# A gated recurrence into a gated feed-forward layer: y transposed by TensorE for all slabs, the cap as minimum and maximum, and a new order of all steps

## The chip, the cores and the metric

The kernel runs on one core of a Trainium2 chip. Its time is device microseconds of one execution. A second execution was taken by the hardware profiler; all rows below come from that one.

## The reference, cut to what matters

There are 4 batches, 8 heads, 768 time steps and 48 values a head. Each head has a complex state of 48 x 48 that decays by a complex factor for each row, and takes up the outer product of k and v:

```
mag = sqrt(a_re^2 + a_im^2);  scale = minimum(mag, 0.999) / (mag + 1e-6)
ar, ai = a_re * scale, a_im * scale
for t in range(768):
    S_re, S_im = ar[t] * S_re - ai[t] * S_im + outer(k[t], v[t]),  ar[t] * S_im + ai[t] * S_re
    y[t] = q[t] @ S_re
x   = y as (3072 tokens, 384)
out = (sigmoid(x @ w_gate) * (x @ w_val)) @ w_out      # 384 -> 1536 -> 384, float32
```

## The kernel before, in words

**Tiling.** Time is cut into six chunks of 128 steps. A *slab* m is one chunk c of one batch b, with all 8 heads: 128 time steps on the partitions, 384 columns; m counts 4c + b, so there are 24. Slabs come in seven groups (`SIZES`: 4, 4, 4, 4, 4, 2, 2), which share the steps on the decays; slabs come in pairs w = m // 2 for the feed-forward layer.

**The steps of a group and a slab**, by the names that the planner uses. Decays: `lr`, `la` load a_re and a_im; `sq`, `add` give the squared magnitude, `lnm` its logarithm, `lh` the cap. In groups 2 to 6 (`SPLIT`) `lh` caps the logarithm and writes a float16 high part (line 631), and `ll` on VectorE the remainder (line 640); in groups 0 and 1 the cap comes before the logarithm (line 622). `cl` sums the logarithms over time by a matmul with a triangle, `ee` takes exponentials, `scr` and `rbe` carry the last row's decay through memory, `arr` multiplies it. Angles: `lna`, `inv`, `r`, `atan`, `hop`, `th`, `tl`, then sums by `ct`, rounding by `r16` and `nid`, and `cr`, `ab`, `cs` for carry, cosine and sine. Products: `lk`, `lq`, `lv` load k, q, v; `v16` and `qke` scale them; `ks`, `qs` turn them by the angles. For slabs 9 to 23 (`CROSSED`) `xk` and `xq` transpose them by a crossbar DMA (line 881), for the others `tp` on TensorE and `qkT`, a copy. `sc` makes scores, `mst` masks them, `u`, `x16`, `kv`, `P` carry the state, and `y` (lines 995 and 997) puts both parts together in a bank of PSUM.

**Around the change.** `y16` (lines 1008 to 1011) copies y to float16. Then the feed-forward layer wants it transposed, in a tile `xt` of the pair. For slabs in `YCROSSED`, 4 to 23, step `xt` is a crossbar DMA from SP's queue (line 1016). For the others `xp` makes three 128 x 128 transposes on TensorE into a bank (line 1029) and `xt` copies them out, on VectorE or ScalarE (line 1035). When both slabs of a pair have their `xt`, `pg` and `pv` multiply by w_gate and w_val (line 1054, twelve matmuls for a block of 256 hidden columns, six each), `tanh` and `p` gate, `po` multiplies by w_out (line 1093), `ot` copies out, `st` stores.

**What sets the order.** A planner wrote it out beforehand: `TIMES` has a due time for each step, `Plan.order` sorts all steps by it, and every engine carries out its own steps in that order; a step that waits holds all that stand behind it on its engine. The due times are the planner's numbers, and no measurement. SP issues all loads, `scr`, `rbe`, `car`, the crossbar DMAs and the stores in one queue; the weights and `hop` are issued by GpSimd. `HOME` names the engine of a step that has a choice (v VectorE, a ScalarE, g GpSimd), one letter a slab or pair; `SLOTS` says which of a few buffers each tile gets, the eight banks of PSUM (`ps`) among them. `WARM` puts dummy matmuls of zeros ahead of some TensorE steps (line 1132). Activation tables are loaded where the next function needs another set.

Of the kernel before, what the change touches and what calls it, by code (L numbers as in the profile page):

```python
# [10 lines left out]
ALU = mybir.AluOpType  # L11
# [17 lines left out]
YCROSSED = range(4, 24)  # L29
# [5 lines left out]
    "sq": "aaavvvvaavaaaaaaavvaaaaa",  # L35
    "add": "vgvvvggggggggggggggggggg",
    "lh": "vgvgggggggvg",
    "r": "vvgggvgggggv",
    "v16": "ggavgvggvggvggaggaavvavv",
    "qke": "vggggggggggggggggggggggg",  # L40
    "th": "aaaaggggvgav",
    "ab": "vavvvaaavvavaavaaaaaavva",
    "u": "ggggggggggggggvggggg",
    "x16": "gagggggaggagggva",
    "y16": "aavvvavaavvvaaaavavvvvvv",
    "xt": "vvvavvvvvvvvvvvvvvvvvvvv",
    "ot": "vvavvvvaavvaaavvaavvaaaaa",
# [17 lines left out]
    "sq": [
        4.48, 10, 6.32, 8.16, 17.85, 17.86, 21.38, 29.97, 51.59, 50.73, 56.79,
        63.29, 82.29, 91.4, 88.28, 87.26, 107.64, 104.58, 114.27, 114.29,
        147.67, 152.47, 176.52, 173.69],
    "add": [
        7.2, 10.92, 7.68, 9.03, 19.38, 20.6, 30.47, 32.67, 56.38, 63.25,  # L70
        65.53, 66.21, 87.89, 92.17, 90.8, 88.18, 110.42, 111.34, 128.31,
        116.63, 162.03, 164.86, 177.13, 178.13],
    "lna": [
        11.97, 33.75, 64.73, 92.51, 117.97, 165.5, 180.57],
    "lh": [
        11.96, 9.67, 20.61, 32.68, 69.79, 70.41, 97.82, 98.99, 132.8, 140.86,
        165.93, 180.53],
    "lnm": [
        13.56, 33.16, 66.22, 93.79, 129.94, 165.92, 179.6],
    "inv": [  # L80
        12.16, 33.76, 70.86, 106.34, 117.98, 166.8, 181.9],
    "r": [
        16.38, 13.68, 37.9, 37.89, 74.86, 73.97, 108.49, 109.1, 118.24,
        134.35, 172.6, 183.16],
    "cl": [
        15.08, 16.37, 19.88, 20.63, 33.77, 38.14, 39.84, 33.97, 77.53, 79.36,
        71.95, 78.08, 101.69, 105.47, 107.63, 106.65, 138.38, 138.71, 143.08,
        142.1, 168.69, 170.09, 197.48, 195.63],
    "ee": [
        19.39, 19.87, 20.58, 21.37, 37.16, 43.83, 41.98, 37.17, 81.07, 81.68,  # L90
        72.77, 82.28, 102.22, 107.65, 109.34, 108.48, 140.04, 143.11, 144.33,
        143.41, 169.29, 172.61, 201.81, 196.64],
# [73 lines left out]
    "mst": [  # L166
# [215 lines left out]
def kernel(  # L382
# [184 lines left out]
    for g, n in enumerate(SIZES):  # L567
# [595 lines left out]
```

## Time and profile before

| | us |
|---|---|
| median of 3 runs | 315.61 (314.3 to 316.31) |
| profiled execution | 316.14 |
| its span, first to last instruction | 314.4 |
| TensorE matmuls busy | 237.2 (75%) |
| VectorE busy | 207.1 (66%) |
| ScalarE busy | 200.6 (64%) |
| GpSimd busy | 147.8 (47%) |

The mean granted clock of TensorE is 0.908 of full speed. Busy time is a share of the whole span; in the rows, PE is TensorE, PEld its weight loads, DVE VectorE, ACT ScalarE, POOL GpSimd, SPq the sequencer that issues DMAs. "out<-in" names tiles by the program's names. A time in brackets is how long the engine stood idle before the row, and what ended it.

### The profile page before, as it was taken

What the parts mean: (1) busy time and instruction counts of PE and PEld (TensorE: products, weight loads), DVE (VectorE), ACT (ScalarE), POOL (GpSimd) and SP (SyncE); (2) the same over time, 40 slices, a digit from 0 to 9 for tenths busy, and PEclk for the clock granted to TensorE, in tenths of its full rate; (3) what the DMA queues carried; (4) which work ended last, traced back from release to release, by engine and by line L of the source; (5) the groups of instructions that cost most, each with busy time, mean ns of one, the idle gap of its engine ahead of it and who ended that gap; (6) DMA issues with size and microseconds to landing.
All of it is one profiled execution on the core that took longest, in us unless ns stands there. A gap on an engine that the chain in (4) does not pass through costs nothing.

```text
span 314.4 us, 5826 instructions
## 1 busy us (share of the span) xinstructions
PE 237.2 (75%) x2178; PEld 175.5 (56%) x2178; DVE 207.1 (66%) x334; ACT 200.6 (64%) x313; POOL 147.8 (47%) x140
## 2 busy tenths in 40 slices
PE   0094899995997937598968649779759699779396
PEld 0042766794674626366845427547547477467284
DVE  3569998994887737477978628648626469567131
ACT  3688997797677945579877719568556376512032
POOL 3218773499754579627299443057214350240000
PEclk9998799999599996979999959887969789979989
DMA  8999969969957593693994799394493618263401
GB/s 160 217 214 193 202 91 164 139 115 151 203 98 152 125 174 71 129 190 87 216 163 94 116 177 220 74 177 100 87 205 75 142 25 183 57 124 83 125 2 52
DMA packets 191309, 42.24 MB, mean 134 GB/s; under 512 B 184200, under 2 KB 191280, under 8 KB 191280
## 3 DMA queue, kind: packets, MB, share of 16 engines
q1 hardware_dynamic: 187136, 38.29, 64.4%
q0 software_dynamic: 4144, 3.56, 7.9%
q8 instruction: 17, 0.28, 0.4%
q14 instruction: 12, 0.10, 0.1%
HBM read 30.77 MB, written 4.78 MB: 113 GB/s over the span
## 4 chain that ended last, share of the span: by engine, by line
PE 26%; DMA 12%; SPq 6%; DVE 4%; issue 3%; POOL 3%; ACT 3%; DVEq 0%; POOLq 0%; ACTq 0%
PE banks L1054 15%; PE banks L1093 6%; DMA xt<-y 4%; DMA rbe<-scr 3%; DMA qkT<-kst 2%; SPq L561 2%; SPq L1016 2%; PE banks L922 2%; SPq L881 1%; DMA out_dram<-ot 1%; DMA a<-in_a_im_dram 1%; DVE p L1072 1%; DVE mst L937 1%; DVE y L523 1%; POOL state L951 1%
## 5 line engine op out<-in xcount | busy, mean ns | idle before, releaser
L1054 PE MATMUL banks<-xt,wg 128*128 128x256 f16 x432 | 63.3, 295 | 20.0 <-DMA xt<-y 15.9
L1065 ACT ACTIVATE g<-banks 128x512 f16<-128x512 f32 x72 | 42.0, 596 | 45.1 <-PE banks L1054 35.7
L1054 PE MATMUL banks<-xt,wv 128*128 128x256 f16 x432 | 64.6, 295 | 4.6 <-DMA xt<-y 3.9
L1054 PEld LDWEIGHTS <-wg 128*128 128x128 f16 x432 | 44.3, 105 | 33.1 <-issue 19.1
L732 POOL TENSOR_TENSOR qk<-qk,ee 128x768 f32<-128x768 f32 x23 | 43.6, 1896 | 40.2 <-DMA qk<-in_q_dram 23.8
L1072 DVE SCALAR_TENSOR_TENSOR p<-g,banks 128x512 f16<-128x512 f16 x72 | 48.0, 681 | 17.9 <-ACT g L1065 12.4
L1093 PE MATMUL banks<-wo,p 128*128 128x384 f16 (+1 forms) x300 | 56.2, 327 | 0.0
L1054 PEld LDWEIGHTS <-wv 128*128 128x128 f16 x432 | 44.7, 106 | 19.6 <-issue 7.4
L937 DVE TENSOR_TENSOR mst<-banks,msk_t 128x512 f16<-128x512 f32 x48 | 32.2, 684 | 22.9 <-PE banks L922 21.4
L1126 ACT ACT_TABLE_LOAD x31 | 39.8, 1283 | 0.5
L1093 PEld LDWEIGHTS <-p 128*128 128x128 f16 x300 | 28.5, 100 | 15.0 <-issue 1.2
L860 DVE TENSOR_TENSOR kst<-qk,banks 128x768 f16<-128x768 f32 x24 | 22.7, 947 | 8.6 <-POOL qk L732 7.8
L600 POOL TENSOR_TENSOR lm<-sq 128x384 f32<-128x384 f32 x20 | 20.7, 1039 | 16.4 <-ACT sq L592 10.1
L922 PEld LDWEIGHTS <-qkT 128*128 128x128 f16 x192 | 15.1, 108 | 23.7 <-DMA qkT<-kst 12.2
L592 ACT ACTIVATE sq<-a 128x768 f32<-128x768 f32 x17 | 14.4, 845 | 15.4 <-DMA a<-in_a_im_dram 10.7
L860 DVE TENSOR_TENSOR qst<-qk,banks 128x768 f16<-128x768 f32 x24 | 22.7, 945 | 0.0
L922 PE MATMUL banks<-qkT,qkT 128*128 128x128 f16 x120 | 12.6, 244 | 12.3 <-DMA qkT<-kst 10.5
L631 POOL TENSOR_SCALAR lh<-lm 128x768 f16<-128x768 f32 x7 | 19.4, 2780 | 3.7 <-ACT lm L613 3.5
L679 ACT ACTIVATE ee<-banks 128x384 f32<-128x384 f32 x24 | 11.8, 492 | 12.6 <-PE banks L671 11.4
L667 PE MATMUL banks<-lm,wl_t 128*128 128x384 f32 x16 | 7.9, 612 | 15.6 <-ACT lm L613 15.6
L656 POOL TENSOR_TENSOR a<-a 128x768 f32<-128x768 f32 x8 | 15.3, 1925 | 5.8 <-ACT a L650 5.8
L807 DVE TENSOR_SCALAR r<-banks 128x384 f16<-128x384 f32 x24 | 13.1, 551 | 6.7 <-PE banks L792 6.6
(91 smaller groups left out, 407.4 us busy)
## 6 DMA issues: line engine op xcount, KB each, us to landing
a<-in_a_re_dram SPq DMA_DIRECT2D x24, 192.0 KB
a<-in_a_im_dram SPq DMA_DIRECT2D x24, 192.0 KB
v<-in_v_dram SPq DMA_DIRECT2D x24, 192.0 KB
qk<-in_k_dram SPq DMA_DIRECT2D x24, 192.0 KB
qk<-in_q_dram SPq DMA_DIRECT2D x24, 192.0 KB
out_dram<-ot SPq DMA_DIRECT2D x23, 192.0 KB
wg<-in_moe_w_gate_dram POOLq DMA_DIRECT2D x3, 384.0 KB, 6.5
wv<-in_moe_w_val_dram POOLq DMA_DIRECT2D x3, 384.0 KB, 5.3
```

The lines of the kernel that those rows point to most:

```text
L600: home("add", m).tensor_tensor(out=T[LM][:, s], in0=T[SQ][:, 0], in1=T[SQ][:, 1], op=ALU.add)
L631: home("lh", w).tensor_scalar(out=T[LH][:, 0, i:j], in0=T[LM][:, i:j], scalar1=LNCAP, scalar2=1.0, op0=ALU.min, op1=ALU.mult)
L656: home("r", w).tensor_tensor(out=T[A][:, 1, i:j], in0=T[A][:, 1, i:j], in1=T[A][:, 0, i:j], op=ALU.mult)
L732: home("qke", m).tensor_tensor(out=T[QK], in0=T[QK], in1=T[EE], op=ALU.mult)
L860: nc.vector.tensor_tensor(out=T[SL][i].rearrange("p h (r x) -> p h r x", r=2)[:, :, :, 0:D], in0=heads(T[QK][:, i]).unsqueeze(2) .broadcas ...
L922: nc.tensor.matmul(sc[:, 4 * hf * both + i], kt, qt, start=True, stop=True)
L937: nc.vector.tensor_tensor(out=T[MS][:, :n_], in0=T[SC], in1=msk_t.unsqueeze(1).broadcast_to([L, n_, L]), op=ALU.mult)
L1054: nc.tensor.matmul(T[ACC][:, r], wt[:, j, f0:f0 + 128], T[XT][:, :, j], start=(j == 0), stop=(j == 2))
L1065: nc.scalar.activation(out=T[G16], in_=T[PG], func=FT.Tanh, scale=0.5)
L1072: nc.vector.scalar_tensor_tensor(out=T[PT][:, 2 * fp:2 * fp + 2], in0=T[G16], scalar=1.0, op0=ALU.add, in1=T[PV], op1=ALU.mult)
L1093: nc.tensor.matmul(T[PO][:, :wd], T[PT][:, fb, s0:s0 + L], wo16[:, fb, c0:c0 + wd], start=(fb == 0), stop=(fb == NFB - 1))
L1126: nc.scalar.preload_act_table_set(SETS[key[1]])
```

## The change

The range of slabs whose y goes by the crossbar becomes empty, so slabs 4 to 23 take the two steps that slabs 0 to 3 had. The cap of the split groups does a minimum with the logarithm's limit and then a maximum with -200 in place of a multiplication by 1. Homes, due times, buffers and dummies of all steps are new: 37 dummies in place of 26, other slabs for most homes, and the last group (slabs 22, 23) now ends before the one of slabs 20, 21.

```diff
-YCROSSED = range(4, 24)
+YCROSSED = ()
 HOME = {
...
-    "lh": "vgvgggggggvg",
+    "lh": "gvgggggvvggv",
...
-    "y16": "aavvvavaavvvaaaavavvvvvv",
-    "xt": "vvvavvvvvvvvvvvvvvvvvvvv",
+    "y16": "vaavavvvaavvavvvaaaaaaaa",
+    "xt": "vvavvvvvavvvvvvavavaavav",
...
 TIMES = {
...
     "y": [
-        34.81, 41.97, 39.99, 45.62, 66.83, 67.24, 81.71, 88.4, 100.63, 105.59,
-        110.39, 114.91, 136.7, 137.43, 151.36, 150.3, 165.49, 168.28, 178.14,
-        177.15, 201.18, 201.82, 215.25, 217.61],
+        35.34, 52.95, 39.91, 41.45, 65.88, 66.29, 85.49, 85.97, 103.07,
+        106.19, 121.6, 118.72, 132.83, 136.14, 152.51, 152.46, 168.42, 166.57,
+        182.06, 183.12, 217.78, 216.07, 201.29, 205.6],
...
     "xp": [
-        37.3, 42.95, 45.44, 49.24],
+        44.07, 56.12, 42.3, 42.62, 68.09, 69.89, 88.51, 88.68, 108.61, 108.44,
+        123.73, 124.6, 135.27, 138.5, 156, 156.01, 170.3, 170.13, 184.83,
+        184.99, 219.5, 219.88, 205.59, 205.67],
     "xt": [
-        37.75, 43.32, 45.48, 49.61, 70.42, 70.43, 84.3, 91.38, 103.71, 108.47,
-        117.28, 117.29, 138.62, 139.05, 153.27, 153.28, 168.9, 170.11, 180.62,
-        180.79, 203.15, 205.16, 218.68, 218.75],
+        44.44, 57.32, 43.28, 44.11, 69.86, 70.69, 89.51, 89.61, 109.11,
+        109.53, 124.78, 125.88, 137.6, 138.93, 156.04, 156.51, 171.79, 171.81,
+        187.61, 187.64, 219.87, 220.19, 205.64, 205.97],
...
 WARM = {
-    ('sc', 0, 1): 3,
-    ('sc', 1, 1): 1,
-    ('kv', 2): 1,
-    ('kv', 1): 1,
-    ('sc', 4, 1): 1,
-    ('pg', 0, 2): 9,
-    ('kv', 4): 5,
-    ('sc', 7, 0): 5,
+    ('ct', 3): 8,
+    ('ct', 1): 1,
+    ('sc', 0, 0): 4,
+    ('sc', 0, 1): 10,
+    ('y', 0): 2,
+    ('pv', 1, 0): 4,
+    ('pv', 1, 3): 1,
+    ('cl', 10): 7,
 }
...
             def e2(T, LM=LM, LH=LH, i=i, j=j, w=w):
                 home("lh", w).tensor_scalar(
                     out=T[LH][:, 0, i:j], in0=T[LM][:, i:j], scalar1=LNCAP,
-                    scalar2=1.0, op0=ALU.min, op1=ALU.mult)
+                    scalar2=-200.0, op0=ALU.min, op1=ALU.max)
```

## Rows read from the trace of the kernel before

**Rows 1.** The page: busy time and instructions of TensorE, granted clock in tenths.
```profile
PE 237.2 (75%) x2178; PEld 175.5 (56%) x2178; DVE 207.1 (66%) x334; ACT 200.6 (64%) x313; POOL 147.8 (47%) x140
...
PEclk9998799999599996979999959887969789979989
```

**Rows 2.** Busy time by stretch: from:to, length, each engine's busy us, clock, DMA.
```profile
45.00:314.40 269.40, 213.62 (x2016) 160.06 (x2014) 173.30 (x269) 165.21 (x267) 124.23 (x109) 0.90 0.69 127
```

**Rows 3.** The waits: who waited for whom, us in total, times, longest.
```profile
PE banks L1054 <- DMA xt<-y: 19.8, 8, 4.8
...
PE banks L922 <- DMA qkT<-kst: 10.5, 4, 5.4
...
DVE lh L640 <- POOL lh L631: 6.7, 3, 3.7
...
PE banks L922 <- DMA qkT<-qst: 1.8, 1, 1.8
```

**Rows 4.** Busy time by stretch: from 79.7, 202.6, 246.9, 277.6 and 298.1, summed.
```profile
sum 24.00, PE 22.38 PEld 15.08 DVE 12.79 ACT 11.78 POOL 6.83; mean PE 4.48 PEld 3.02 DVE 2.56 ACT 2.36 POOL 1.37
```

**Rows 5.** Busy time by stretch: four more at half clock.
```profile
117.20:124.00 6.80, 4.47 (x36) 3.29 (x36) 6.23 (x9) 3.27 (x5) 6.49 (x7) 0.50 0.50 109
134.30:137.70 3.40, 3.04 (x17) 1.73 (x16) 2.30 (x5) 2.45 (x5) 0.80 (x1) 0.50 0.91 166
182.10:188.90 6.80, 3.56 (x17) 2.38 (x18) 2.12 (x3) 1.72 (x4) 3.91 (x4) 0.50 0.98 198
229.90:236.70 6.80, 5.16 (x37) 3.97 (x38) 3.00 (x6) 4.29 (x6) 1.26 (x2) 0.50 1.00 200
```

**Rows 6.** The chain that ended last, in order of time: start, us, what.
```profile
256.29 1.31 PE banks L1054 x12
...
273.56 3.20 DMA xt<-y
```

**Rows 7.** Timeline from 39.9 to 41: start, us, engine, line, operation.
```profile
40.10 0.33 PE L1029 MATMUL banks<-idn_t,y 128*128 128x128 f16 x3
...
40.27 0.22 PE L1132 MATMUL banks<-zero 128*128 128x128 f16 x1
...
40.55 0.34 DVE L530 COPY xt<-banks 128x384 f16<-128x384 f16 x1
```

**Rows 8.** Timeline from 291 to 298: the last slab's y and y16.
```profile
291.28 0.18 PE L997 MATMUL banks<-v,mst 128*128 128x48 f16 x1
...
294.14 0.56 DVE L523 TENSOR_SCALAR ot<-banks 128x384 f32<-128x384 f32 x1 [3.47 <-DMA out_dram<-ot]
...
294.62 0.55 DVE L523 TENSOR_SCALAR y<-banks 128x384 f16<-128x384 f32 x1
```

**Rows 9.** Groups by line and shape: count, busy us, mean ns, idle before.
```profile
L631 POOL TENSOR_SCALAR lh<-lm 128x768 f16<-128x768 f32 x7 | 19.4, 2780 | 3.7 <-ACT lm L613 3.5
...
L523 POOL TENSOR_SCALAR a<-a 128x768 f16<-128x768 f32 x5 | 4.2, 832 | 2.8 <-DMA a<-car 2.4
...
L622 POOL TENSOR_SCALAR lm<-lm 128x768 f32<-128x768 f32 x2 | 1.6, 823 | 7.0 <-DVE lm L600 6.9
```

**Rows 10.** Timeline from 73 to 81: the caps of group 2.
```profile
73.75 5.54 POOL L631 TENSOR_SCALAR lh<-lm 128x768 f16<-128x768 f32 x2
...
79.33 1.29 DVE L640 SCALAR_TENSOR_TENSOR lh<-lm,lh 128x768 f16<-128x768 f32 x1 [3.70 <-POOL lh L631]
```

**Rows 11.** Timeline from 113 to 134: a cap, and loads held behind y.
```profile
113.72 2.78 POOL L631 TENSOR_SCALAR lh<-lm 128x768 f16<-128x768 f32 x1
...
116.54 0.96 DVE L640 SCALAR_TENSOR_TENSOR lh<-lm,lh 128x768 f16<-128x768 f32 x1 [2.39 <-POOL lh L631]
...
117.77 0.57 SPq L561 DMA_DIRECT2D v<-in_v_dram  x1
...
119.27 0.58 PE L922 MATMUL banks<-qkT 128*128 128x128 f16 x4 [4.26 <-DVE qst L860]
...
126.11 1.19 SPq L1016 DMA_TRANSPOSE xt<-y  x1
...
131.36 1.04 DVE L594 TENSOR_TENSOR sq<-a 128x768 f32<-128x768 f32 x1 [4.08 <-DMA a<-in_a_re_dram]
...
133.33 0.32 PE L671 MATMUL banks<-lh,wl 128*128 128x384 f16 x1 [3.73 <-DVE lh L640]
```

More of the change, by code (lines that the diff above doesn't have):

```diff
@@ L34 @@
 HOME = {
-    "sq": "aaavvvvaavaaaaaaavvaaaaa",
-    "add": "vgvvvggggggggggggggggggg",
-    "lh": "vgvgggggggvg",
[L38 to L44, printed above, removed]
-    "y16": "aavvvavaavvvaaaavavvvvvv",
-    "xt": "vvvavvvvvvvvvvvvvvvvvvvv",
-    "ot": "vvavvvvaavvaaavvaavvaaaaa",
+    "sq": "vaaavvvaaaaaaaavaaaaaaaa",
+    "add": "vgvvgggggggggggggggggvgg",
+    "lh": "gvgggggvvggv",
+    "r": "vvgggggggggv",
+    "v16": "ggggggvvggggggagvvvavagv",
+    "qke": "gggvggggggggggggggggvggg",
+    "th": "aaaavgggvgav",
+    "ab": "vaavvaaavaaavvaaaaaaaavv",
+    "u": "ggggggggggggggggvvvv",
+    "x16": "gggvgaagggvavggg",
+    "y16": "vaavavvvaavvavvvaaaaaaaa",
+    "xt": "vvavvvvvavvvvvvavavaavav",
+    "ot": "avvvaavvavaaavavaavavaaav",
 }
@@ L51 @@
     "wg": [
-        33.15, 33.98, 55.11],
+        28.88, 44.09, 23.19],
     "wv": [
-        38.84, 40.48, 56.42],
+        31.95, 49.27, 52.96],
     "wo": [
-        66.18, 71.97, 66.17],
+        74.01, 69.87, 76.44],
     "lr": [
-        0.75, 7.71, 4.49, 7.69, 12.18, 13.57, 17.87, 22.94, 36.42, 46.49,
-        56.39, 59.16, 76.9, 89.89, 81.08, 82.27, 98.5, 104.43, 108.45, 111.37,
-        140.84, 145.45, 171.53, 171.54],
+        0.75, 10.04, 8.57, 1.12, 10.05, 13.69, 19.93, 24.8, 44.13, 57.38,
@@ L61 @@
+        60.18, 62.71, 70.64, 78.81, 78.82, 70.65, 101.57, 120.18, 117.75,
+        117.48, 166.56, 168.43, 133.38, 151.46],
     "la": [
-        1.12, 9.04, 4.5, 7.7, 17.82, 17.83, 16.39, 25.79, 43.6, 36.43, 56.35,
-        59.17, 81.7, 89.9, 84.94, 84.29, 105.6, 99.37, 111.38, 110.41, 140.85,
-        152.46, 172.58, 171.55],
+        1.49, 10.03, 8.56, 8.08, 13.7, 10.06, 15.09, 30.65, 47.51, 55.33,
+        60.17, 62.72, 70.68, 76.47, 78.45, 78.83, 102.43, 102.49, 117.76,
+        107.79, 167.59, 169.97, 134.14, 150.84],
@@ L72 @@
-        116.63, 162.03, 164.86, 177.13, 178.13],
+        8.07, 12.17, 9.54, 8.55, 19.27, 23.18, 31.71, 31.73, 57.18, 63.7,
+        66.74, 66.92, 78.78, 80.37, 92.65, 85.96, 116.2, 126.77, 120.19,
+        123.7, 174.48, 175.13, 150.64, 154.3],
     "lna": [
-        11.97, 33.75, 64.73, 92.51, 117.97, 165.5, 180.57],
+        10.75, 32.78, 65.3, 92.67, 122.97, 176.29, 156.77],
     "lh": [
-        11.96, 9.67, 20.61, 32.68, 69.79, 70.41, 97.82, 98.99, 132.8, 140.86,
-        165.93, 180.53],
+        12.18, 10.02, 31.66, 31.96, 70.62, 71.44, 98.38, 107.93, 127.81,
@@ L78 @@
+        132.62, 179.91, 158.47],
     "lnm": [
-        13.56, 33.16, 66.22, 93.79, 129.94, 165.92, 179.6],
+        13.71, 32.8, 67.09, 92.7, 127.39, 176.21, 155.21],
     "inv": [
-        12.16, 33.76, 70.86, 106.34, 117.98, 166.8, 181.9],
+        12.16, 32.79, 66.3, 92.68, 123.68, 186.68, 160.83],
     "r": [
-        16.38, 13.68, 37.9, 37.89, 74.86, 73.97, 108.49, 109.1, 118.24,
-        134.35, 172.6, 183.16],
+        14.55, 13.68, 35.36, 35.47, 70.36, 69.88, 102.45, 97.5, 132.59,
+        136.16, 188.77, 175.22],
@@ L96 @@
-        154.25, 183.18, 183.17, 205.1, 205.13],
+        32.77, 40.65, 33.65, 41.29, 56.14, 54.7, 49.68, 54.71, 97.53, 88.7,
+        86.74, 98.31, 120.16, 123.71, 120.2, 119.68, 150.82, 156.06, 154.25,
+        145.08, 191.39, 191.37, 187.65, 179.98],
     "rbe": [
-        54.17, 58.94, 98.46, 130.11, 157.86, 187.32, 205.17],
+        57.33, 57.39, 98.35, 123.74, 159.31, 200.77, 187.66],
     "lk": [
-        20.62, 29.51, 20.96, 23.5, 30.48, 36.69, 53.32, 60.01, 76.89, 84.28,
-        85.77, 86.4, 93.2, 123.09, 120.49, 95.7, 121.36, 151.42, 141.24,
@@ L102 @@
-        137.4, 176.04, 151.4, 180.63, 166.81],
+        19.92, 32.76, 24.68, 21.22, 45.82, 32.81, 49.69, 49.67, 70.66, 86.77,
+        88.69, 98.36, 98.32, 109.16, 125.87, 124.61, 143.56, 98.4, 144.41,
+        150.81, 154.27, 187.62, 166.15, 179.69],
     "lq": [
-        23.1, 31.98, 23.52, 23.51, 38.15, 39.85, 56.36, 60.02, 81.09, 84.95,
-        91.41, 96.88, 117.96, 125.88, 120.5, 127.13, 130.79, 151.43, 157.87,
-        152.44, 187.31, 173.7, 180.65, 205.11],
+        24.69, 36.86, 30.66, 21.81, 47.5, 42.79, 57.37, 56.15, 76.46, 89.5,
@@ L107 @@
+        97.49, 98.41, 98.34, 117.95, 133.31, 124.81, 146.68, 149.99, 166.12,
+        152.53, 174.3, 193.31, 179.92, 187.68],
     "lv": [
-        31.95, 20.59, 36.44, 42.78, 59.77, 12.17, 77.55, 61.32, 72.27, 81.92,
-        96.89, 102.25, 114.94, 121.37, 150.11, 147.86, 155.68, 130.12, 122.17,
-        155.52, 176.06, 190.9, 172.19, 205.14],
+        23.15, 40.64, 24.67, 33.18, 63.3, 65.89, 76.45, 78.84, 86.76, 97.54,
+        100.02, 114.29, 97.52, 133.34, 133.35, 133.82, 157.18, 163.85, 145.05,
@@ L111 @@
+        143.75, 196.08, 185.51, 185.52, 201.23],
     "v16": [
-        34.27, 27.47, 37.88, 43.59, 66.19, 17.84, 78.09, 78.11, 75.81, 105.48,
-        102.67, 110.4, 114.95, 134.36, 150.35, 148.48, 164.87, 139.04, 170.08,
-        172.17, 198.91, 201.19, 208.54, 205.15],
+        23.16, 44.12, 31.69, 40.2, 65.29, 65.9, 81.57, 82.21, 102.48, 97.55,
+        117.03, 117.49, 117.74, 135.3, 138.51, 140.52, 158.46, 164.82, 174.26,
+        166.14, 200.58, 212.8, 200.59, 203.07],
     "qke": [
-        23.11, 33.17, 25.8, 25.81, 47.96, 54.2, 56.81, 69.78, 81.67, 86.41,
@@ L117 @@
-        92.49, 97.81, 120.06, 125.91, 129.18, 131.24, 147.83, 153.25, 157.91,
-        162.06, 191.53, 181.46, 202.82, 205.12],
+        24.7, 38.63, 31.7, 21.82, 47.52, 49.28, 58.49, 57.34, 83, 92.66,
+        98.39, 99.11, 114.28, 120.21, 133.32, 130.11, 149.81, 154.26, 166.17,
+        170.31, 207.38, 195.9, 186.67, 192],
     "atan": [
-        16.4, 39.86, 75.4, 111.35, 135.98, 174.75, 186.64],
+        17.67, 37.87, 70.84, 102.47, 140.28, 188.79, 179.95],
     "ct": [
-        17.81, 22.28, 19.4, 20.95, 40.68, 43.82, 47.95, 56.34, 81.69, 81.91,
@@ L128 @@
-        157.85, 188.76, 186.65, 200.73, 203.57],
+        20.74, 23.98, 21.21, 22.55, 40.66, 44.71, 49.29, 55.35, 80.39, 82.99,
+        93.51, 96.84, 111.3, 117.78, 130.73, 123.75, 145.86, 150.03, 163.24,
+        163.84, 205.61, 200.81, 185.68, 186.66],
     "nid": [
-        19.5, 24.45, 22.93, 23.09, 43.34, 47.35, 54.61, 58.93, 82.89, 84.92,
-        96.34, 92.93, 120.47, 121.99, 129.93, 131.94, 147.66, 152.42, 155.51,
-        158.81, 189.39, 187.28, 201.59, 205.09],
+        21.8, 28.01, 24.81, 23.14, 41.28, 45.8, 52.13, 55.54, 81.38, 84.69,
@@ L133 @@
+        93.94, 97.48, 111.5, 118.2, 131.37, 127.38, 146.89, 150.63, 163.89,
+        166.75, 205.66, 201.64, 186.46, 187.63],
     "cr": [
-        24.46, 29.98, 27.49, 27.53, 43.84, 47.83, 56.37, 61.97, 84.97, 86.39,
-        98.47, 94.87, 122.81, 123.58, 131.95, 133.31, 151.38, 153.57, 156.8,
-        160.32],
+        23.2, 35.46, 25.06, 24.66, 42.8, 49.24, 57.19, 57.35, 84.66, 91.36,
+        97.58, 99.61, 114.27, 120.17, 132.12, 130.09, 149.01, 154.24, 166.76,
+        169.5],
     "ab": [
-        19.86, 32.66, 23.96, 24.44, 43.81, 51.58, 56.41, 61.96, 84.93, 85.29,
@@ L144 @@
-        162.08, 192.85, 188.78, 203.69, 205.94],
+        23.89, 36.85, 31.72, 25.46, 45.01, 49.25, 58.48, 57.36, 84.67, 91.38,
+        98.37, 99.62, 114.32, 120.96, 132.6, 130.1, 150.83, 154.28, 166.77,
+        171.8, 205.95, 203.08, 188.29, 192.65],
     "ks": [
-        24.91, 33.74, 27.51, 30, 47.97, 54.21, 58.49, 69.8, 86.36, 89.05,
-        100.17, 97.86, 124.37, 126.23, 132.81, 138.39, 152.45, 156.54, 160.28,
-        162.09, 195.42, 190.88, 205.91, 208.53],
+        24.79, 39.92, 31.74, 26.65, 48.59, 49.66, 59.54, 57.59, 84.68, 93.5,
@@ L149 @@
+        98.44, 99.97, 116.18, 120.97, 134.13, 132.13, 151.57, 157.16, 167.58,
+        174.28, 207.39, 203.34, 191.35, 193.83],
     "qs": [
-        25.78, 35.21, 27.52, 30.46, 47.98, 54.62, 58.51, 69.81, 87.23, 89.91,
-        101.71, 98.1, 125.36, 127.1, 133.3, 138.4, 152.6, 156.55, 160.33,
-        162.69, 195.43, 190.89, 205.92, 208.55],
+        25.66, 39.93, 31.75, 28, 49.26, 51.13, 66.73, 61.47, 85.39, 93.95,
+        99.1, 102.21, 116.21, 121.61, 136.15, 132.14, 152.44, 157.17, 169.49,
@@ L255 @@
     "x16": [
-        64.77, 61.31, 77.87, 72.95, 100.04, 105.49, 108, 98.97, 134.4, 136.72,
-        147.85, 144.06, 164.85, 168.1, 177.14, 158.84],
+        63.33, 65.27, 84.64, 78.47, 102.51, 99.99, 116.84, 118.7, 132.63,
+        134.22, 149.79, 141.37, 166.55, 166.16, 179.94, 163.93],
     "ll": [
-        76.02, 71.52, 97.84, 105.45, 136.71, 140.87, 168.12, 192.83],
+        74.05, 76.48, 104.57, 107.94, 128.29, 136.72, 179.93, 158.59],
     "car": [
-        74.88, 105.46, 141.25, 172.18],
+        70.35, 107.59, 135.28, 174.27],
@@ L270 @@
-        172.16, 171.58, 195.46, 192.82, 208.52, 210.17],
+        100.01, 115.54, 108.63, 125.23, 133.39, 145.06, 141.16, 158.49,
+        161.61, 171.77, 174.31, 211.51, 204.33, 194.71, 199.92],
     "xq": [
-        97.85, 107.66, 109.11, 130.8, 132.16, 141.26, 143.42, 158.82, 162.04,
-        165.91, 171.57, 195.64, 192.84, 208.51, 208.94],
+        101.56, 109.14, 108.62, 124.8, 133.33, 142.26, 140.53, 158.5, 160.84,
+        173.62, 175.23, 211.52, 205.93, 196.07, 199.93],
 }
@@ L276 @@
     "a2": "0101010",
[L277 removed]
+    "sq": "010101010101101001011010",
     "lm": "0101010",
[L279 to L285 removed]
@@ L286 @@
-    "v16": "012345623140523401625041",
-    "r16": "010010101010101010100101",
-    "ee": "012330213210213021302130",
-    "qk": "012340213402134201043231",
-    "cr": "01010",
-    "qkT": "012345012305140523140523142503251403251403152415",
-    "mst": "012301230123120312031203120303120213021302131302",
-    "y16": "012021012012012010210120",
-    "xt": "012102102102",
-    "g16": "0120120210212120112012012021021201121201020101212012012021021020"
-        "10120200",
-    "p": "012021201021",
-    "x16": "01201020201020101202",
+    "ps": "0124360267667014577016455062347235625432452450140675407654765467"
+        "4654501506174012340732067540132601450361243054232365726473262016"
+        "3210230145671036452016720742647326304310240126241532402140540674"
+        "5167542346574260340523654132120515046750712032543064723627627620"
+        "1376210245610270126512350245612045106746742350624567156400402346"
+        "7237606234162172620164327601756",
@@ new lines @@
+    "ee": "012313203210230123101302",
+    "qk": "012340321043210243042310",
+    "r16": "010010100101101001011010",
+    "v32": "012112021022102101220121",
+    "v16": "012345603124506132451603",
+    "cr": "01010",
+    "qkT": "012345012534013425340125342501342501340125013401",
+    "mst": "012301120312230101230123230123010213120303121203",
+    "y16": "012021021021012101210210",
+    "xt": "012012012012",
+    "g16": "0120121012102120211201220120012101120122121201210210102001221022"
+        "02102120",
```

68 lines of the change are left out of this document (28 added, 40 removed), and 142 rows, old and new, of the table TIMES.

## The prediction, made before the changed kernel ran

> **What bounds the kernel now.** The first view is the page's busy times and its clock line: TensorE is the busiest engine and still works only three quarters of the span, and its granted clock sags in many slices [rows 1]. The second is the busy time by stretch: after the first 45 us, which fill the pipeline, TensorE works 213.62 of 269.40 us and idles 55.8 [rows 2]. So the end is set by TensorE's work plus its stalls, and the question is who ends them. The waits name them [rows 3]: 19.8 us in 8 waits end when a crossbar transpose of y lands, 12.3 in 5 when one of k or q lands; VectorE waits 6.7 in 3 for the caps (`lh`) on GpSimd. The fourth view, the granted clock by stretch, shows what a stall costs afterwards: five stretches of together 24.00 us that follow stalls ended by y's transpose run at the lower level, 1.2 in place of 2.4 GHz [rows 4], and of four more, one follows a late cap, one a held load and two the transposes of k and q [rows 5].
>
> **The change, part by part.** Durations are of the profiled execution, whose own time is 316.14 us around a span of 314.4; that is 0.5 above the median of 315.61.
>
> *Twenty crossbar transposes leave the SP queue; slabs 4 to 23 go y16, `xp`, `xt`.* A transfer of y takes about 3.2 us from issue to landing [rows 6]. The TensorE way, which slabs 0 to 3 use already, took from 40.10 to 40.89: three transposes in 0.33 and a copy of 0.34 with the handoffs [rows 7], so 0.78. Eight waits keep 0.78 each: 19.8 - 6.2 = 13.6 comes back. The last of them does not belong to the transfer alone: y16 of the last slab stood behind an output copy on VectorE [rows 8], so I take 12. The bounds are 0 (whatever made y late stays late) and 13.6.
>
> *The clock.* In the five stretches TensorE is busy 22.38 us at half speed [rows 4]; all of it at full speed would be worth 11.2. Stalls left elsewhere will cool it again, so I take half, 5.6; bounds 0 and 11.2.
>
> *The cap becomes minimum, then maximum.* Seven caps on GpSimd cost 2.78 us each [rows 9]. The same engine does minimum and maximum on as many elements in 0.82 with a float32 result, and two multiplications with a float16 result in 0.83 [rows 9]; between these stands the new form, so 0.83. It is on the path: two caps in a row hold `ll` on VectorE 3.70 us [rows 10], and the cap that ends at 116.50 holds it 2.39, behind which the products for slab 8 stand, and TensorE waits 4.26 until 119.27 [rows 11]. Five caps instead of seven stay on GpSimd and three instead of one go to VectorE, whose `ll` on as many elements takes 0.96 [rows 11]. Of VectorE's 6.7 I take 5, and half of the 2.2 that full clock would save in the stretch from 117.2 [rows 5]: 6 together. Bounds: 0, if the next wait swallows it, and 8.9.
>
> *Loads no longer stand behind y.* SP issues in order and waits at `xt` until y16 is there: after the load at 117.77 it issues nothing until 126.11. The a load behind it then makes VectorE wait 4.08 for its squares, `ll` is queued behind them, and TensorE waits 3.73 for `cl` [rows 11]. That wait goes: 3.7, and half of the 1.5 in the clock stretch from 134.3 [rows 5]: 4.5; bounds 0 and 5.2. The remaining SP steps keep such holds: k's and q's transposes wait for VectorE there as before, and in three groups the read-back `rbe` now directly follows the last `scr`, so SP stands there until that lands. I take nothing for it: most loads are issued several steps ahead of their use; for one that isn't, the price is a wait like the 4.08 above.
>
> *TensorE's own new work.* Sixty transposes. From the first of three to the next instruction 0.17 passes, to the end of the third 0.33 [rows 7]: 3.4 to 6.6 in all. Eleven more dummies cost from 0.06 (the third of that 0.17) to the 0.22 of one alone, each: 0.6 to 2.4. Most stand in a filled queue, so 5 of bounds 4 and 9. The Trainium skill speaks against this part: VectorE: DVE Perf Modes, section The three transpose paths, gives 390 ns for one 128x128 transpose on TensorE (and 1309 for the crossbar). By that figure the sixty would cost 23.4, an estimate, and the sum would come out at 314. The trace has three in 0.33, so I stay with it.
>
> *The copy behind each transpose* is 0.34 on VectorE [rows 7]; 14 of the 20 new ones lie there, 6 on ScalarE. Both engines have over 100 us of idle time, which hides them; without that cover a copy costs its length on the way to `pg`, which the 0.78 holds already.
>
> *New waits at `xp`.* It stands in TensorE's own queue, so a late y16 holds every matmul behind it, where before it held SP. By the new order, with 0.65 for six matmuls of the gate or value product [rows 6] and other steps likewise, the work between y and `xp` is 0.8 to 5.5 us, 1.95 in the middle of the twenty. The worst row of before outside the held loads is the last slab: y's last matmul ends at 291.46, y16 at 295.17, 3.7 later [rows 8]; against the 0.8 that slab 23 has now, that is 2.9. I take 3, for one such case; the low end is 0.
>
> *The rest of the new order*: squares, decays, copies of v and state move one or two each between engines that idle a third of the time; the new buffers' order gives TensorE's banks twenty more users. Groups 5 and 6 change places, and the program ends with slab 21's whole store where half a store closed; the copy in it is at most the 0.55 of its nearest row [rows 8]. I take nothing for either; the bounds are in the rivals.
>
> **Sum**: -12 - 5.6 - 6 - 4.5 + 5 + 3 = -20.1; 316.1 - 20.1 = 296.
>
> **The rivals.**
> 1. *All comes back.* Every cost at its good end: -13.6 - 11.2 - 8.9 - 5.2 + 4 = -34.9, so 281. For it: a TensorE that doesn't stall isn't slowed. Against: k's and q's stalls stay and cool it. 14 in 100 for under 290.
> 2. *The wait moves to k's and q's transposes.* These thirty stay on SP behind the same VectorE. TensorE already waits 12.3 for them [rows 3]. If the new order doubles that, with 4.4 for a clock that falls again (half of TensorE's 3.56 and 5.16 in the stretches from 182.1 and 229.9 [rows 5]), the gain shrinks by 16.7 to 313. For it: with y's waits gone they are what is late next, for `sc`. Against: SP has 20 fewer steps, each of which held it. 15 in 100, of which 9 end within 1%.
> 3. *Slower: TensorE stalls at `xp`.* Its place is the gap between y and y16, now in TensorE's queue; its price is 3.7 of lag [rows 8] less 1.95 of cover, 1.75 for each of twenty slabs, 35: 296 - 3 + 35 = 328. It decides from 1.1 us a slab on (22 us over twenty). For it: 14 y16 instead of 10 go to ScalarE, behind its tables and activations. Against: that lag was VectorE waiting for an output buffer. 14 in 100 for anything that ends over 1% slower.
> 4. *The cap stays slow.* No row shows minimum and maximum with a float16 result. Then five caps of 2.78 stay on GpSimd and five sevenths of the 6 are lost: 300. 7 in 100.
> 5. *Transposes don't overlap.* Each takes the 0.22 that a single matmul of that shape shows [rows 7]: 13.3 for 5, so 304. The page quoted above would have it still dearer; what stands there speaks against both. 3 in 100.
>
> The forecast itself, 290 to 304, has 47 in 100. A measurement of this kernel tells about 1% from no change. Faster by more: 47 + 14 + 7 + 3 + 6 = 77; within: 9; slower: 14. The range reaches from rival 1 to beyond rival 2, 281 to 317, and leaves out the slower case and a few in 100 below.
>
> **What would show it.** In the changed kernel's trace: no crossbar transpose of y, 24 triples of TensorE transposes; caps on GpSimd near 0.83; TensorE idle after 45 us near 30 in place of 55.8; fewer stretches at the lower clock; no SP gap of seven microseconds ahead of a load. It would be wrong if TensorE's waits at `xp` for y16 come to over 20 us, if the waits for k's and q's transposes double, or if the same idle time returns under other names.

## The result: 260.4 us, faster than the forecast's range

The changed kernel takes 260.39 us (median of 4 runs, 259.69 to 261.05) against 315.72 (4 runs, 314.3 to 316.31): a ratio of 0.8253, 95% interval 0.8213 to 0.8292. The forecast was 296 with a range of 281 to 317. The direction was right, the size wrong by 36 us: 55 came off where 20 were forecast. Here and below a median is of all runs of a kernel, and a ratio of its fast runs alone, which leaves out single executions some per cent slower than the others.

The profile of the changed kernel, page lines for busy time and granted clock (its span is 258.0 us, its own time 259.69):

```profile
PE 218.9 (85%) x2249; PEld 168.2 (65%) x2249; DVE 210.4 (82%) x345; ACT 200.8 (78%) x323; POOL 131.0 (51%) x137
...
PEclk9999689999999999999999999999999999999999
```

Against [rows 1] VectorE and ScalarE do the same work as before within 2%, in a shorter span; GpSimd's 16.8 us less are mostly the caps. The clock line has its only dip while the pipeline fills. By stretch (from:to, length, each engine's busy us, clock, DMA), the answer to [rows 2]:

```profile
45.00:258.00 213.00, 197.89 (x2101) 154.55 (x2096) 179.85 (x288) 166.61 (x281) 106.04 (x102) 1.00 0.84 152
```

TensorE idles 213.00 - 197.89 = 15.1 us where it idled 55.8, and is busy 197.89 where it was busy 213.62. The two differences, 40.7 and 15.7, are the whole 56.4 by which the span fell. The waits of the changed kernel (who waited for whom, us in total, times, longest), the answer to [rows 3]:

```profile
PE banks L671 <- ACT lm L617: 15.5, 1, 15.5
PE banks L907 <- DVE qst L864: 4.6, 1, 4.6
PE banks L818 <- DVE r L811: 2.8, 3, 1.3
...
PE banks L999 <- POOL x L534: 1.7, 1, 1.7
...
PE banks L926 <- DMA qkT<-qst: 1.2, 2, 0.6
...
PE banks L926 <- DMA qkT<-kst: 0.4, 1, 0.4
```

The first two lie in the filling. Of what follows, y's 19.8 us are gone with their transfers. The waits for the transposes of k and q are the surprise: those thirty steps are still there, and the waits fell from 12.3 to 1.6 us. Neither `xp` (TensorE's transposes, L1033) nor the cap is among TensorE's waits. The other 10.2 of the 40.7 (40.7 - 19.8 - 10.7) is the net of all other waits. The groups that are new or changed (count, busy us, mean ns, idle before and who ended it), the answer to [rows 7, 9]:

```profile
L1033 PE MATMUL banks<-idn_t,y 128*128 128x128 f16 x72 | 6.9, 219 | 0.0
...
L534 DVE COPY xt<-banks 128x384 f16<-128x384 f16 x17 | 5.9, 351 | 2.7 <-PE banks L1033 2.6
...
L635 POOL TENSOR_SCALAR lh<-lm 128x768 f16<-128x768 f32 x5 | 4.4, 886 | 2.6 <-ACT lm L617 2.5
```

All 72 transposes of y take 6.9 us of TensorE, which is idle 0.0 us ahead of them, and a cap takes 886 ns in place of 2780.

### The profile page after: what moved, and what is told of

It is laid out like the page before. It is cut to its first block, busy times and chain, and to the rows that moved or that the text cites. A ratio compares the mean times of both kernels' runs of the same rounds, so it can differ in the third digit from the quotient of the medians.

```text
span 258.0 us, 5947 instructions
## 1 busy us (share of the span) xinstructions
PE 218.9 (85%) x2249; PEld 168.2 (65%) x2249; DVE 210.4 (82%) x345; ACT 200.8 (78%) x323; POOL 131.0 (51%) x137
## 4 chain that ended last, share of the span: by engine, by line
PE 29%; DVE 17%; ACT 17%; DMA 16%; issue 8%; SPq 7%; POOL 4%; DVEq 0%; ACTq 0%; POOLq 0%
PE banks L1058 12%; PE banks L1097 8%; ACT L1130 4%; DMA qk<-in_q_dram 4%; DMA a<-in_a_re_dram 3%; DVE p L1076 3%; DMA qkT<-qst 3%; SPq L565 3%; ACT g L1069 3%; DMA v<-in_v_dram 3%; DVE mst L941 2%; SPq L698 2%; DVE kst L864 2%; PE banks L671 2%; DVE qst L864 2%
## 5 line engine op out<-in xcount | busy, mean ns | idle before, releaser
L1058 PE MATMUL banks<-xt,wv 128*128 128x256 f16 x432 | 57.2, 272 | 1.8 <-ACT ot L525 0.9
L1058 PE MATMUL banks<-xt,wg 128*128 128x256 f16 x432 | 55.9, 272 | 1.4 <-DVE p L1076 0.6
L736 POOL TENSOR_TENSOR qk<-qk,ee 128x768 f32<-128x768 f32 x22 | 41.9, 1921 | 13.5 <-DMA qk<-in_q_dram 10.9
L1058 PEld LDWEIGHTS <-wv 128*128 128x128 f16 x432 | 41.0, 98 | 10.0 <-issue 3.6
L1058 PEld LDWEIGHTS <-wg 128*128 128x128 f16 x432 | 41.3, 98 | 9.3 <-issue 2.9
L596 ACT ACTIVATE sq<-a 128x768 f32<-128x768 f32 x19 | 16.0, 847 | 8.0 <-DMA a<-in_a_im_dram 4.4
L926 PEld LDWEIGHTS <-qkT 128*128 128x128 f16 x192 | 13.5, 98 | 7.0 <-issue 3.9
L671 PEld LDWEIGHTS banks<-lm,wl_t 128*128 128x128 f32 x16 | 3.6, 250 | 19.5 <-ACT lm L617 16.5
L828 ACT ACTIVATE cr<-banks 32x384 f32<-32x384 f32 x20 | 9.7, 483 | 8.5 <-DVE banks L843 8.2
L907 PE MATMUL banks<-idn_t,kst 128*128 128x128 f16 x72 | 10.4, 229 | 6.7 <-DVE qst L864 4.6
```

The costliest lines, as they stand in the source:

```text
L596: on.activation(out=T[SQ], in_=T[A][:, :, s], func=FT.Square)
L671: nc.tensor.matmul(T[CL][:, :HD], wl_t, T[LM][:, s], start=True, stop=True)
L736: home("qke", m).tensor_tensor(out=T[QK], in0=T[QK], in1=T[EE], op=ALU.mult)
L1058: nc.tensor.matmul(T[ACC][:, r], wt[:, j, f0:f0 + 128], T[XT][:, :, j], start=(j == 0), stop=(j == 2))
```

## The experiments

The theory after the result, which the experiments test: **SP carries out its steps in order, and y's crossbar step at the head of them was a cause that the waits listed under other names.** While it waits for y16 nothing behind it is issued, neither k's and q's transposes nor loads; those come late, TensorE stalls for them, and its clock falls. The rival theories: the new order, not the queue, brought the extra; the cap did; or the crossbar's own traffic was what slowed k's and q's transfers. All times below are medians of interleaved runs, and ratios are to the kernel before on the same chip, where it took 313.8 to 315.3.

### The parts one by one

**e1_before_y_on_pe**: the kernel before, order, engines and cap unchanged, with y on TensorE.

```
-YCROSSED = range(4, 24)
+YCROSSED = ()
...
+EXTRA = {
+    "xp_4": 2, "xp_5": 2, "xp_6": 6, "xp_7": 6, "xp_8": 6,
...
```

Cut here: `xp` gets the due times that `xt` had (slab 6: 87.251 for 84.3), and `EXTRA` gives its twenty new users their banks.

> The kernel before with one part of the change: slabs 4 to 23 go y16, xp, xt on TensorE, at the due time that the crossbar transfer had (slab 6 three planner units later, where a bank is free); order, homes, dummies and cap as before. Queue theory (y's step on SP held loads and the transposes of k and q, and TensorE's idle time and its lower clock came from that): near 275, TensorE idle after 45 us under 30. Order theory (the new due times are what paid; this part is worth what the prediction gave it, some 18): near 298. Cap theory (the slow caps held the chain): over 300.

Measured: 277.85, ratio 0.8868 [0.8787, 0.895]. Its stretch after 45 us:

```profile
45.00:277.80 232.80, 204.78 (x2076) 157.35 (x2074) 185.55 (x289) 164.01 (x267) 126.57 (x109) 0.97 0.78 138
```

and its waits:

```profile
PE banks L677 <- DVE lh L646: 4.8, 3, 2.0
...
PE banks L1035 <- DVE y L529: 1.4, 1, 1.4
...
PE banks L928 <- DMA qkT<-qst: 0.6, 1, 0.6
```

Moving y alone brings 37 of the 55 us. Nothing was done to k's and q's transposes, and TensorE's waits for them go from 12.3 to 0.6, as they would if they had been held behind y. Idle time is 28.0, and the clock 0.97.

**e2_before_new_cap**: the kernel before with the new cap alone.

```
-                    scalar2=1.0, op0=ALU.min, op1=ALU.mult)
+                    scalar2=-200.0, op0=ALU.min, op1=ALU.max)
```

> The kernel before with the cap as minimum and maximum, nothing else. Cap theory: 290 or less. Queue and order theories: 305 to 312, for the 6 us or so that the caps' waits on VectorE and TensorE come to; caps near 0.83 on GpSimd in all of them.

Measured: 313.15, ratio 0.9999 [0.9953, 1.0044]. Its groups:

```profile
L631 POOL TENSOR_SCALAR lh<-lm 128x768 f16<-128x768 f32 x7 | 5.7, 823 | 3.4 <-ACT lm L613 3.2
L640 DVE SCALAR_TENSOR_TENSOR lh<-lm,lh 128x768 f16<-128x768 f32 x8 | 10.6, 1322 | 0.0
```

its waits:

```profile
PE banks L1054 <- DMA xt<-y: 22.3, 8, 4.8
```

and its stretch after 45 us:

```profile
45.00:312.50 267.50, 209.42 (x1997) 157.56 (x1997) 174.48 (x267) 164.12 (x265) 109.16 (x108) 0.92 0.68 127
```

GpSimd is 13.7 us less busy in its caps, and VectorE's 6.7 us of waiting for them are gone (idle ahead of L640: 0.0). TensorE idles 58.1 all the same, 2.3 more than before, and y's waits grew from 19.8 to 22.3. TensorE's busy time is 4.2 lower than in [rows 2], so the span of this one execution is 1.9 shorter; over the timed runs nothing is left of it. What the cap gave up on VectorE shortened no stall of TensorE; 2.5 us more are put down to y. The numbers expected were too low.

**e7_before_y_on_pe_new_cap**: e1 with the new cap, the same two words edited.

> The kernel before with y on TensorE and the new cap, order and homes as before. With y gone from SP the caps are what is late next: the cap is worth 3 to 10 us here (it was worth nothing alone), 268 to 275; the order then gives the rest to 260. If the cap stays worth nothing without the new order: 278.

Measured: 270.67, ratio 0.8586 [0.8522, 0.8651]; after 45 us TensorE idles 23.3 (223.40 - 200.09). The cap that brought nothing in e2 brings 7.2 (277.85 - 270.67) once y is off SP.

**e3_after_y_crossed**: the kernel after with y's slabs 4 to 23 back on SP, at the due times of `xp` (slabs 9 and 17 0.171 later), and the buffer order of PSUM's banks without the twenty `xp`. The cut edit:

```
-YCROSSED = ()
+YCROSSED = range(4, 24)
```

> The kernel after with y's crossbar transposes back on SP for slabs 4 to 23, each at the due time of its xp; order, homes and cap of the kernel after. Queue theory: 295 to 310, with TensorE idle near 50 after 45 us and the lower clock back. Order theory: under 275. Latency alone (3.2 us a transfer in place of 0.8, on the way to pg, with no hold): 270 to 280.

Measured: 320.09, ratio 1.0235 [1.0122, 1.0348]: 60 us dearer than with y on TensorE, and dearer than any of the numbers expected. TensorE's waits:

```profile
PE banks L917 <- DMA qkT<-kst: 17.6, 5, 8.4
PE banks L1049 <- DMA xt<-y: 10.8, 5, 4.1
...
PE banks L917 <- DMA qkT<-qst: 2.8, 2, 1.6
```

The larger part of the listed waits is k's and q's (20.4), not y's (10.8). The step that waits is not the step that holds.

**e8_after_order_alone** (e3 with the old cap: the new order and nothing else) and **e4_after_old_cap** (the kernel after with the old cap):

```
-                    scalar2=-200.0, op0=ALU.min, op1=ALU.max)
+                    scalar2=1.0, op0=ALU.min, op1=ALU.mult)
```

Expected of e8, and then of e4:

> The new order, homes and dummies alone: y crossed on SP and the old cap. Queue theory: as the crossed version with the new cap, 318 to 326, since a cap that is faster behind a held queue gains nothing. If the cap matters in the new order whatever the queue does: over 326.

> The kernel after with the cap as minimum and multiplication by 1. Five caps on GpSimd at 2.78 in place of 0.89, 9.5 us of GpSimd time. Cap theory: 280 or more. Queue and order theories: 262 to 269, the caps' extra time as far as VectorE waits for it.

Measured: e8 320.16, ratio 1.0208 [1.0169, 1.0247]; e4 263.86, ratio 0.8427 [0.8348, 0.8506]. In e4 the group of caps:

```profile
L635 POOL TENSOR_SCALAR lh<-lm 128x768 f16<-128x768 f32 x5 | 14.2, 2842 | 2.6 <-ACT lm L617 2.5
```

The slow cap is fully there and costs 3.5 us of the end (263.86 - 260.39). The eight combinations (medians; the first beside e1):

| | y on SP, old cap | y on SP, new cap | y on TensorE, old cap | y on TensorE, new cap |
|---|---|---|---|---|
| old order | 314.6 | 313.2 | 277.9 | 270.7 |
| new order | 320.2 | 320.1 | 263.9 | 260.4 |

The new order loses 6 to 7 us with y on SP and wins 10 to 14 without. The cap wins 0 to 1 with y on SP, which the interval of e2 doesn't tell from none, and 3 to 7 without. Only y's step wins by itself: 37 to 42 in the old order, 56 to 60 in the new one.

### What of y's step on SP costs

These start from the kernel after, where y goes through TensorE, and put twenty transfers back on SP that nobody reads. What they cost cannot be a transfer that `pg` waits for.

**e5_after_and_idle_transfers**: each waits for its y16, at the due time of its `xp`, and writes one unused tile.

```
+    unused = const.tile([L, 3, L], F16, name="unused")
...
+            if m >= 4:
+                def e(T, Y16=Y16):
+                    nc.sync.dma_start_transpose(out=unused, in_=T[Y16])
+
+                add(("xd", m), e, after=[("xp", m)], use=[Y16])
```

> The kernel after, with twenty crossbar transposes added on SP: each reads the y16 of a slab from 4 on, at the due time of its xp, and writes to a tile that nobody reads. So SP waits for y16 as it did before, but no transfer of y is on the way to pg. Queue theory: most of the loss of the crossed version comes back, 285 to 315. Latency theory (the transfer's 3 us on the way to pg is what costs): under 268.

Measured: 328.72, ratio 1.0442 [1.0371, 1.0513], more than in e3, whose transfers are read. The one unused tile adds a wait of its own, as the next run shows: each transfer must see the one before it landed.

**e6_after_and_transfers_that_wait_for_nothing**: as e5, with a constant tile for the source, so that SP waits for no y16.

```
-                    nc.sync.dma_start_transpose(out=unused, in_=T[Y16])
+                    nc.sync.dma_start_transpose(out=unused, in_=still)
```

> As the run with idle transfers, but the twenty read a constant tile of the same size, so that SP does not wait for y16. What is left is 20 issues of 1.2 us and the traffic. If the wait for y16 holds the queue: 261 to 268. If the transfers themselves disturb (issue time, crossbar among the loads): as much as the run with idle transfers, over 280.

Measured: 286.48, ratio 0.9123 [0.9093, 0.9153]. SP's waits show the fault of the experiment:

```profile
SPq L1044 <- DMA unused<-still: 13.1, 9, 2.4
```

These waits are the experiment's, not y's, so neither size stands. The next two have four unused tiles in turn and are otherwise e5 and e6.

**e9_idle_transfers_four_tiles**:

```
-    unused = const.tile([L, 3, L], F16, name="unused")
+    unused = [const.tile([L, 3, L], F16, name=f"unused{i}") for i in range(4)]
...
+                    nc.sync.dma_start_transpose(out=unused[m % 4], in_=T[Y16])
```

> As the run with idle transfers of y16, but written to four tiles in turn, so that no transfer waits on SP for the one before it (12.1 us in 8 waits there); the waits for y16 stay. If the waits for y16 hold the queue: 310 to 326. If the waits among the transfers were what cost: under 290.

Measured: 316.27, ratio 1.0095 [1.0045, 1.0144]. Transfers that nobody reads cost 56 us, as much as the change had gained. Its stretch after 45 us, and two around the place shown below:

```profile
45.00:313.90 268.90, 211.71 (x2110) 160.43 (x2108) 184.08 (x290) 167.28 (x280) 104.36 (x102) 0.93 0.69 128
...
139.00:146.00 7.00, 0.39 (x6) 0.21 (x4) 1.22 (x2) 0.97 (x3) 4.78 (x4) 0.85 0.62 131
146.00:152.00 6.00, 5.97 (x33) 3.82 (x34) 2.02 (x4) 2.73 (x6) 1.02 (x2) 0.61 1.01 202
```

Both parts of the gain are lost again: TensorE idles 57.2 us (268.90 - 211.71) where the changed kernel idles 15.1, and is busy 13.8 longer, with its clock at 0.93. TensorE's waits:

```profile
PE banks L929 <- DMA qkT<-kst: 17.1, 3, 7.9
PE banks L1105 <- ACT g L1077: 6.7, 1, 6.7
...
PE banks L929 <- DMA qkT<-qst: 5.4, 2, 3.1
```

Part of the loss comes by loads. ScalarE's squares wait 10.2 us for loads of a_re, where those of the changed kernel wait 2.1, and the longest of these waits stands ahead of the gate (`g`) for which TensorE waits 6.71; the wait as it is listed, then the two rows of the timeline:

```profile
ACT sq L599 <- DMA a<-in_a_re_dram: 10.2, 4, 6.8
...
94.18 0.84 ACT L599 ACTIVATE sq<-a 128x768 f32<-128x768 f32 x1 [6.76 <-DMA a<-in_a_re_dram]
...
96.32 1.44 PE L1105 MATMUL banks<-wo,p 128*128 128x384 f16 x4 [6.71 <-ACT g L1077]
```

One such place in the timeline of e9 (start, us, engine, line, operation, idle time before and who ended it):

```profile
130.77 0.44 SPq L568 DMA_DIRECT2D a<-in_a_im_dram  x1
...
138.33 0.50 ACT L528 ACTIVATE y<-banks 128x384 f16<-128x384 f32 x1
...
138.85 2.50 SPq L1042 DMA_TRANSPOSE unused<-y  x2
...
141.45 1.25 SPq L888 DMA_TRANSPOSE qkT<-qst  x1
...
142.75 1.34 SPq L888 DMA_TRANSPOSE qkT<-kst  x1
...
146.03 0.61 PE L929 MATMUL banks<-qkT,qkT 128*128 128x128 f16 x4 [6.64 <-DMA qkT<-kst]
```

Four things follow one another. SP issues nothing for 7.6 us, from 131.21 to 138.85, when y16 is done. Then two transfers that nobody reads go out, and k's and q's transposes behind them. TensorE, which computes 0.39 us in seven, waits 6.64 "for k". And in the stretch behind the stall its clock is 0.61. In the list of TensorE's waits, no transfer of y is to be found.

**e10_transfers_that_wait_for_nothing_four_tiles**: e9 with the constant source.

```
-                    nc.sync.dma_start_transpose(out=unused[m % 4], in_=T[Y16])
+                    nc.sync.dma_start_transpose(out=unused[m % 4], in_=still)
```

> As the run with transfers of a constant tile, but written to four tiles in turn: the 13.1 us in 9 waits of SP for the transfer before it are gone, and what is left is 20 issues of 1.2 us and the traffic of 20 transposes. Queue theory: 262 to 272, the added 24 us of issue on SP costing little. If traffic or issue time costs: 278 or more, near the 286 of the run with one tile.

Measured: 277.15, ratio 0.8868 [0.8795, 0.894]. The issues on SP (ns least, median, most; first and last start):

```profile
L1044 SPq DMA_TRANSPOSE unused<-still x20: 1197/1248/2925, 68.1 to 250.5; - x20
```

TensorE's waits:

```profile
PE banks L931 <- DMA qkT<-qst: 5.5, 2, 3.9
...
PE banks L931 <- DMA qkT<-kst: 4.6, 4, 2.3
```

Without the wait for y16 the twenty cost 16.8 us, and the wait accounts for 39 (316.3 - 277.2). The buffer of y16, which a transfer of e9 also holds until it lands, is no way by which it costs: no engine's wait in e9 is put down to one of these transfers. The 16.8 are more than the queue theory allowed; either the 25 us of SP that the issues take (20 x 1.25) cost them, or the crossbar's traffic does. The last two tell those apart.

**e12_small_transfers_that_wait_for_nothing**: e10 with a third of the data.

```
-                    nc.sync.dma_start_transpose(out=unused[m % 4], in_=still)
+                    nc.sync.dma_start_transpose(out=unused[m % 4][:, 0],
+                                                in_=still[:, :L])
```

> As the transfers of a constant tile to four tiles in turn, but each transposes 128 of the 384 columns: a third of the traffic, the same number of issues. If the issue time on SP (20 of 1.2 us) makes the 17 us by which the large ones were slower than the kernel after: 274 to 279. If the traffic does: 264 to 268.

Measured: 276.31, ratio 0.8807 [0.8714, 0.8901]. The issues:

```profile
L1044 SPq DMA_TRANSPOSE unused<-still x20: 1120/1224/1652, 68.0 to 248.3; - x20
```

A third of the data is issued in the same time and costs the same. So it isn't the amount of data.

**e13_plain_copies_that_wait_for_nothing**: e10 with three plain copies of a third each in place of one crossbar transpose.

```
-                    nc.sync.dma_start_transpose(out=unused[m % 4], in_=still)
+                    for j in range(3):
+                        nc.sync.dma_start(unused[m % 4][:, j],
+                                          still[:, j * L:(j + 1) * L])
```

> As the transfers of a constant tile to four tiles in turn, but as three plain copies of 128 columns each in place of one transpose: 60 copies at 0.3 to 0.5 us of issue, 18 to 30 us on SP in all, the same bytes, no crossbar. If SP's issue time makes the 17 us: 272 to 280. If the crossbar transposes themselves do: 260 to 266.

Measured: 288.1, ratio 0.9169 [0.9067, 0.9271]. The issues:

```profile
L1045 SPq DMA_DIRECT2D unused<-still x60: 476/599/1348, 67.7 to 262.3; - x60
```

TensorE's waits:

```profile
PE banks L931 <- DMA qkT<-kst: 7.6, 5, 2.1
PE banks L931 <- DMA qkT<-qst: 7.3, 2, 4.2
```

No crossbar is used by these, and they cost more: 60 x 0.60 = 36 us of SP for 27.7 of the end, 0.77 for each, beside 16.8 for 25 in e10, 0.67 for each. So the cost goes roughly with SP's time. It goes less well with the number of transfers (0.46 us for each of sixty, 0.84 for each of twenty), and it doesn't need the crossbar. The 288.1 itself is above what either theory was given.

**e11_after_stores_from_scalare**: the kernel after, output stores issued by ScalarE, since SP waits 31 us ahead of them (22.5 and 8.5 in the view of waits).

```
-                        nc.sync.dma_start(out[row:row + L, c0:c0 + wd],
+                        nc.scalar.dma_start(out[row:row + L, c0:c0 + wd],
```

> The kernel after with its 25 stores issued by ScalarE in place of SP, where they wait 31 us for the output copies (22.5 for VectorE's, 8.5 for ScalarE's). Queue theory: SP issues its loads earlier and this is as fast or faster, 254 to 260. Against it: ScalarE pays 25 issues of 0.4 us, 10.5 in all, and waits for VectorE's copies in its own queue: 261 to 270.

Measured: 264.03, ratio 0.8437 [0.8351, 0.8524], 3.6 slower than the kernel after: the number against the queue theory, whose own was 254 to 260. The issues on ScalarE:

```profile
L1119 ACTq DMA_DIRECT2D out_dram<-ot x25: 338/338/413, 95.4 to 258.8; - x25
```

So 31 us of SP's waits were not worth what moving them cost. We read it thus: a hold is dear when something behind it is needed soon, and in the changed kernel little was, with 1.6 us left of TensorE's waits for k and q (0.7 here). This run doesn't show it: the issues take 8.5 us of ScalarE (25 x 0.34), whose price isn't measured apart. No kernel of these beat the changed one.

## Why the prediction was wrong

The failed step is the one headed "Loads no longer stand behind y", with the sentence that the other SP steps keep their holds. It read what the hold costs at one place, [rows 11], and priced it at 4.5 us. The hold was the common cause of most of what came off. By the account of the forecast and of the two traces:

| after 45 us | forecast | measured |
|---|---|---|
| TensorE's idle time | -17.7 (-12 -5 -3.7 +3) | -40.7 |
| lower clock | -7.5 (5.6 + 1.1 + 0.8) | -21.0 |
| TensorE's added work | +5 | +5.3 |
| sum | -20.1 | -56.4 |

The forecast's sum has the cap's two parts rounded to 6. Of the measured column, the idle time and the sum are read from the traces; the clock is an estimate, worked out below, and the added work is what it leaves.

- **y's waits, -12.** All 19.8 are gone, and the landing they ended on was the small part of the cost: e9 has no transfer of y that anybody reads and is as slow as the kernel before. The waits put down to y were one visible end of the hold.
- **Held transfers, -4.5.** The runs put in its place: about 39 us for SP's wait for y16 (e9 less e10) and 17 for SP's time to issue (e10 less the changed kernel), both in the new order. e3 is another 4 above e9, which would be the landing's own price, but their intervals overlap, and e9 still does the transposes on TensorE where e3 doesn't; that price stays open. In the old order the whole step is 37 to 42.
- **k's and q's waits stay; rival 2.** They didn't stay, and rival 2 had the sign wrong: 12.3 became 1.6, and 0.6 in e1. Taking twenty steps off the queue in front of them is what the argument against rival 2 named; the prediction gave it no price.
- **The clock, half.** All of it came back. Before, TensorE was busy at half speed in the nine stretches of [rows 4, 5], for 22.38 + 16.23 us, and in one more, 42.0 in all; the first, that one and the sum of the ten:

```profile
79.70:86.50 6.80, 6.13 (x29) 3.78 (x27) 6.14 (x9) 5.09 (x7) 4.65 (x6) 0.50 1.20 208
...
212.80:216.20 3.40, 3.40 (x19) 2.23 (x17) 2.90 (x5) 2.71 (x4) 3.32 (x4) 0.50 0.58 130
...
sum 51.20, PE 42.01 PEld 28.68 DVE 29.33 ACT 26.23 POOL 22.60; mean PE 4.20 PEld 2.87 DVE 2.93 ACT 2.62 POOL 2.26
```

  By estimate full speed returns half of it, 21.0. Busy time fell by 15.7, so 5.3 were added. The stalls "left elsewhere" that were to cool it again were mostly gone too.
- **The cap, -6.** Its duration was right (0.83 forecast, 0.886 and 0.823 measured; rival 4 falls), its price was not: 0 by itself (e2), 7.2 behind e1, 3.5 in the new order. In e2 VectorE's wait of 6.7 went, and TensorE idled no less.
- **TensorE's new work, +5.** The mechanism held, the size is open: by the group's own busy time sixty are 60/72 of 6.9, or 5.8, while of the 5.3 that the account leaves, 2.6 look like work that the first 45 us no longer hold (TensorE is busy 20.99 there, and was 23.58), which leaves 2.7, below the bounds. The transposes overlap: rival 5 falls. The Trainium skill, VectorE: DVE Perf Modes, section The three transpose paths, has 390 ns for one 128x128 transpose on TensorE. By that figure sixty would be 23.4, an estimate; the trace disagrees, with 5.8 for the sixty.
- **New waits at `xp`, +3; rival 3.** None: TensorE's transposes have 0.0 us of idle time ahead of them.
- **Rival 1, 281.** Nearest, and still 21 too high: it added up the good ends of the terms, and kept k's and q's stalls, which were the queue's part under another name.
- **The order, 0.** Wrong both ways, -10 to -14 with y on TensorE and +6 to +7 without. Which of its edits does it (engines, due times, groups 5 and 6, dummies) stays open; it wasn't tried.

## What to carry to other kernels

Price a DMA step in an in-order queue by all that is queued behind it, its wait for the source and its own issue time, not by the wait that ends when it lands; waits for other transfers of that queue may be the same wait under another name. Where one cause feeds several stalls, take back all of them and the whole of the lower clock, and where it stays, other gains can vanish into it, as the cap's did. Putting the removed step back as an idle copy that nobody reads, with and without its wait, measures hold and issue apart.

## What the runs showed of the hardware

- A GpSimd operation of two steps on 128x768, float32 to float16, takes 2.78 to 2.84 us as minimum and multiplication (before, e4) and 0.82 to 0.89 as minimum and maximum (e2, after).
- A crossbar transpose occupies SP for 1.22 us with 128 columns (e12) and 1.20 to 1.25 with 384 (e3, e9, e10); a plain copy of 128 columns between tiles, 0.60 (e13). These are medians.
- The granted clock stayed at 1.00, its 2.4 GHz level, through 213 us in which TensorE idled 15.1 in pieces, the longest of the listed waits 1.7.
